# Agent attention with a routed expert layer: the planner that spreads side work beside the main tiles also counts GpSimd's instructions

## Chip, cores and metric

One core of a Trainium2 chip runs the whole program. The metric is device time in microseconds (us) of one execution, lower is better.

## What is computed

The reference first does attention through 49 agent vectors, then an expert layer on its output. Sizes: 4 batches of 10048 tokens, width 128; 4 groups of 4 experts, hidden width 1024.

```python
def _attn_ref(q, k, v, agents):
    a2k = sm(agents, k)              # softmax(scale * agents @ k^T), 49 x 10048
    agent_v = a2k @ v
    q2a = sm(q, agents)              # 10048 x 49
    return (q2a @ agent_v)
...
def _moe_ref(x, w_group, w_expert, w1, w2):
    g_logits = x @ w_group
    g_idx = np.argmax(g_logits, axis=1)
...
        e_logits = xg @ w_expert[g]
        e_idx = np.argmax(e_logits, axis=1)
...
            h = np.maximum(xg[mask_e] @ w1[g, e], 0.0)
            ye = h @ w2[g, e]
            combined = g_w[mask_g][mask_e] * e_w[mask_e]
            out[tok_idx] = combined[:, None] * ye
```

## The kernel before, in words

A batch has 79 blocks of 128 tokens. They are worked in **tiles** of 4 blocks (512 tokens), 20 to a batch, by `run`, which takes a tile through eight **units**. A unit is `first` (two matmuls into `ph`, a ScalarE relu into `hh`, and on VectorE the remainder `hl`, since every fp32 value is carried as two fp16 parts) and, eight units later (`LAG`), `second`, twelve matmuls into `po`. At a tile's end VectorE scales `po` into `oo`, and SyncE writes it out. A tile assumes one main expert for the whole batch; the tokens of other experts of the last batch are gathered and done at the end in 17 "taken" tiles (`er`, `ets`, indirect DMA on GpSimd's queue).

All other work is done by generators called **lanes**, which `run` advances between the units of the main tiles. TensorE's instructions from a lane keep the place in which they were written (`pe.pin`); the other engines' are ordered by the scheduler.

- Lane `f` finishes the queries of batch 0 (chunks of 8 blocks), lane `a` makes the agents of the next batch, lane `q` its queries and routing, lane `o` prepares the taken tiles.
- A key chunk in `a` and a query chunk in `q` and `f` begin with `split_load`: ScalarE writes `xh`, the fp16 part of 1024 columns, and GpSimd writes the remainder `xl` in pieces of 256 columns (four instructions a chunk). The scores' matmuls (`agh,xh`, `agl,xh`, `agh,xl`) then need both. There are two buffers each of `xh` and `xl`.
- Later steps of `q` make `rows` (ScalarE, with GpSimd's remainder), of `a` the values (`S`, `sh` and GpSimd's `sl`, VectorE's `vl`). Lane `q` ends with routing, which is VectorE's alone but for a few small matmuls: `oh`, `rm`, `rc`, then the count `cnt`, the main expert's number `mainid`, the loads `w1f` and `w2f`, `output_weight`, and `weights_of`, which fills `wbuf` for the next batch.

How far a lane is driven is decided by counted work. `Counted` wraps an engine and adds to `work[i]`, for each instruction, a fixed cost and a cost per element (nanoseconds, as written by the author). `advance` takes the dot product of what a step added with the weights `WA` and adds it to the lane's `done`; it goes on until `done` reaches the lane's total (`WORK`) times the elapsed part of its span (`SPAN_A`, `SPAN_Q`, `SPAN_F`, in batches: 0.3 is three tenths through batch 0's tiles). GpSimd is not wrapped before the change, so its instructions count nothing.

Of the kernel before, what the change touches and what calls it, by code (L numbers as in the profile page):

```python
# [79 lines left out]
SPAN_Q = {1: (0.53, 0.96), 2: (1.25, 1.78), 3: (2.1, 2.66)}  # L80
SPAN_O = (2.66, 2.92)
SPAN_F = (0.0, 0.52)
WA = (0.3, 1.0, 0.3)
WORK = {"a": 38e3, "q": 42e3, "o": 37.5e3, "f": 38e3}


def const_pack():
# [50 lines left out]

def build(ctx, tc, qT, kT, v, agT, wr, w1, w2, cpk, out):
    nc = tc.nc  # L140
    pool, sync = nc.gpsimd, nc.sync
    work = np.zeros(3)
    pe = Counted(nc.tensor, work, 0, 4.0, 0.42)
    vec = Counted(nc.vector, work, 1, 65.0, 1.04)
    act = Counted(nc.scalar, work, 2, 100.0, 0.83)

    const = ctx.enter_context(tc.tile_pool(name="const", bufs=1))
    stg = ctx.enter_context(tc.tile_pool(name="stg", bufs=4))
# [1060 lines left out]
    def advance(lane, part):  # L1209

        while lane["gen"] and lane["done"] < lane["total"] * part:
# [4 lines left out]
            if x == "end":  # L1216
                lane["gen"] = None
            lane["done"] += float(np.dot(work - w, WA))

    def lane(kind, b, gen, span):  # L1220
        lanes.append(dict(kind=kind, b=b, gen=gen, start=span[0], end=span[1], total=WORK[kind], done=0.0))

# [91 lines left out]
```

## Time and profile before

| | before |
|---|---|
| median of 3 runs (lowest to highest) | 976.26 us (974.47 to 979.38) |
| the profiled execution's own time | 972.96 us |
| its span, first to last instruction | 971.2 us |
| TensorE matmul / weight load, busy | 93% / 75% |
| VectorE, ScalarE, GpSimd, busy | 78%, 65%, 49% |
| mean granted TensorE clock | 0.983 of 2.4 GHz |

Busy shares are of the whole span. A matmul's shown duration includes its way through a pipeline, so TensorE can be shown busy while it starts fewer matmuls than it could; the counts beside the busy times tell that apart.

### The profile page before, as it was taken

What the parts mean: (1) busy time and instruction counts of PE and PEld (TensorE: products, weight loads), DVE (VectorE), ACT (ScalarE), POOL (GpSimd) and SP (SyncE); (2) the same over time, 40 slices, a digit from 0 to 9 for tenths busy, and PEclk for the clock granted to TensorE, in tenths of its full rate; (3) what the DMA queues carried; (4) which work ended last, traced back from release to release, by engine and by line L of the source; (5) the groups of instructions that cost most, each with busy time, mean ns of one, the idle gap of its engine ahead of it and who ended that gap; (6) DMA issues with size and microseconds to landing.
All of it is one profiled execution on the core that took longest, in us unless ns stands there. A gap on an engine that the chain in (4) does not pass through costs nothing.

```text
span 971.2 us, 31446 instructions
## 1 busy us (share of the span) xinstructions
PE 907.4 (93%) x13191; PEld 724.5 (75%) x13191; DVE 762.1 (78%) x1467; ACT 633.3 (65%) x1144; POOL 473.3 (49%) x776
## 2 busy tenths in 40 slices
PE   4979989899999999999889999999899999999996
PEld 3857767687877788887677878877777777777765
DVE  5589988977698987769989776699998766665653
ACT  5467677689757788885668678755455555555542
POOL 4243375388106428620552265300005578888886
PEclk9979989989999999999999999999999999999998
DMA  8863245352048535201883241014503643443311
GB/s 292 236 196 109 84 132 177 107 169 73 24 143 291 169 110 148 64 25 56 283 255 100 81 132 42 24 48 149 164 24 118 216 153 123 129 130 115 121 70 47
DMA packets 104423, 124.58 MB, mean 128 GB/s; under 512 B 6743, under 2 KB 88152, under 8 KB 101328
## 3 DMA queue, kind: packets, MB, share of 16 engines
q1 hardware_dynamic: 99920, 116.57, 38.1%
q0 software_dynamic: 4352, 5.91, 2.2%
q8 instruction: 105, 1.72, 0.7%
q14 instruction: 46, 0.38, 0.1%
HBM read 89.01 MB, written 33.75 MB: 126 GB/s over the span
## 4 chain that ended last, share of the span: by engine, by line
PE 37%; DVE 14%; POOL 4%; DMA 3%; issue 2%; ACT 1%; SPq 0%; POOLq 0%; DVEq 0%; ACTq 0%
PE po L131 19%; PE ph L131 13%; DVE hl L131 6%; PE at L131 6%; DMA xf<-kT 2%; POOL out L1128 1%; POOL er L1091 1%; DVE oo L131 1%; POOL gap L1107 1%; DMA er<-erow,gidx 1%; POOL xl L241 1%; DVE oh L131 1%; DMA wbuf<-wall 1%; DVE oa L131 0%; ACT hh L131 0%
## 5 line engine op out<-in xcount | busy, mean ns | idle before, releaser
L131 DVE SCALAR_TENSOR_TENSOR hl<-ph,hh 128x512 f16<-128x512 f32 (+1 forms) x656 | 435.7, 681 | 134.1 <-ACT hh L131 132.4
L131 PEld LDWEIGHTS <-hh 128*128 128x128 f16 x5200 | 425.3, 98 | 146.2 <-issue 3.3
L131 ACT ACTIVATE hh<-ph 128x512 f16<-128x512 f32 (+1 forms) x656 | 379.5, 594 | 188.2 <-PE ph L131 180.4
L131 PE MATMUL po<-wbuf,hh 128*128 128x128 f16 x4816 | 470.5, 220 | 0.0
L131 PE MATMUL po<-wbuf,hl 128*128 128x128 f16 x2408 | 435.7, 220 | 0.7 <-DVE hl L131 0.7
L131 PE MATMUL ph<-et,wbuf 98*128 98x512 f16 (+1 forms) x1040 | 306.1, 379 | 5.9 <-DVE hl L131 5.1
L241 POOL TENSOR_TENSOR xl<-xf,xh 128x256 f16<-128x256 f32 x292 | 195.6, 702 | 184.8 <-ACT xh L131 182.8
L131 PEld LDWEIGHTS <-hl 128*128 128x128 f16 x2600 | 254.1, 98 | 2.2 <-DVE hl L131 0.9
L1091 POOL DMA_INDIRECT er<-erow,gidx x68 | 69.7, 1025 | 124.5 <-DVE any L131 111.4
L131 PEld LDWEIGHTS <-wbuf 98*128 98x128 f16 x1216 | 94.0, 99 | 22.4 <-issue 12.9
L131 ACT ACTIVATE xh<-xf 128x1024 f16<-128x1024 f32 x80 | 83.2, 1045 | 30.5 <-PE at L131 18.2
L388 POOL TENSOR_TENSOR sl<-S,sh 128x147 f16<-128x147 f32 (+1 forms) x90 | 42.6, 500 | 94.5 <-ACT sh L131 88.4
L1128 POOL DMA_INDIRECT out<-oo,sidx x68 | 67.7, 996 | 23.8 <-DVE oo L131 12.6
L131 PE MATMUL at<-agh,xl 128*128 128x49 f16 x592 | 60.5, 188 | 11.0 <-POOL xl L241 10.1
L610 POOL TENSOR_TENSOR rows<-ef,rows 128x147 f16<-128x147 f32 (+2 forms) x117 | 46.6, 427 | 48.5 <-ACT rows L131 46.5
L131 PEld LDWEIGHTS <-xh 128*128 128x128 f16 x1264 | 60.7, 100 | 11.2 <-ACT xh L131 10.0
L131 PEld LDWEIGHTS <-xl 128*128 128x128 f16 x632 | 53.1, 99 | 16.3 <-POOL xl L241 15.3
L131 PE MATMUL at<-agh,xh 128*128 128x49 f16 x592 | 60.9, 188 | 1.9 <-ACT xh L131 1.7
L131 PE MATMUL at<-agl,xh 128*128 128x49 f16 x592 | 60.6, 188 | 0.0
L131 PE MATMUL ph<-ets,wbuf 98*128 98x512 f16 x176 | 53.1, 385 | 0.8 <-DMA wbuf<-wall 0.8
L1107 POOL MEMSET gap<- 128x320 f16 x136 | 52.4, 385 | 0.3
L131 DVE TENSOR_TENSOR oo<-po,cw 128x512 f32<-128x512 f32 x65 | 44.0, 676 | 5.0 <-PE po L131 5.0
(265 smaller groups left out, 1035.9 us busy)
## 6 DMA issues: line engine op xcount, KB each, us to landing
xf<-kT SPq DMA_DIRECT2D x36, 512.0 KB, 5.6
vf<-v SPq DMA_DIRECT2D x36, 512.0 KB, 5.1
xf<-qT SPq DMA_DIRECT2D x36, 512.0 KB, 4.0
out<-oo SPq DMA_DIRECT2D x62, 256.0 KB, 3.0
wbuf<-wall SPq DMA_DIRECT2D x11, 1024.0 KB, 5.0
wsg<-wall SPq DMA_DIRECT2D x6, 1024.0 KB, 6.8
erow<-rows SPq DMA_DIRECT2D x3, 1975.0 KB, 8.9
w1f<-w SPq DMA_DIRECT2D x7, 512.0 KB, 3.7
```

Of the source, the lines that this page charges most:

```text
L131: y = f(*a, **k)
L241: pool.tensor_sub(out=xl[:, y], in0=xf[:, y], in1=xh[:, y])
L388: pool.tensor_sub(out=sl[0:m, w], in0=x[:, j], in1=sh[0:m, w])
L610: (vec if early else pool).tensor_sub(out=rows[:, w, NA:2 * NA], in0=ef[:, y], in1=rows[:, w, 0:NA])
L1091: ins = pool.indirect_dma_start(out=er[:, q], out_offset=None, in_=erow[b][:, :], in_offset=bass.IndirectOffsetOnAxis(ap=place(b, j * w + ...
L1107: tc.keep_in_program_order(pool.memset(gap, 0.0))
L1128: ins = pool.indirect_dma_start(out=out, out_offset=bass.IndirectOffsetOnAxis(ap=place(x["b"], x["j"] * n + q)[1], axis=0), in_=o[:, q], i ...
```

## The change

GpSimd is wrapped by `Counted` as well (130 ns an instruction and 2.1 ns an element), with weight 0.5 in `WA`. A key chunk's `split_load` then counts for more than its scores, a step of pure VectorE routing for the same as before but against a larger total. The totals of `a`, `q` and `f` are raised; a count made while the program is built gives, as work actually done, 37.4e3 in `a` before and 56.6e3 after, 41.4e3 and 60.6e3 in `q`, 39.6e3 and 52.3e3 in `f`, so each total stands to the work done as it did. Lane `o` has no GpSimd work, and nothing moves in it or behind it. No instruction is added or removed; what moves is when each lane's steps are issued among the units.

```diff
-WA = (0.3, 1.0, 0.3)
-WORK = {"a": 38e3, "q": 42e3, "o": 37.5e3, "f": 38e3}
+WA = (0.3, 1.0, 0.3, 0.5)
+WORK = {"a": 57.4e3, "q": 61.5e3, "o": 37.5e3, "f": 50.2e3}
...
-    pool, sync = nc.gpsimd, nc.sync
-    work = np.zeros(3)
+    sync = nc.sync
+    work = np.zeros(4)
...
+    pool = Counted(nc.gpsimd, work, 3, 130.0, 2.1)
```

The first place is GpSimd (POOL) during batch 0, where lane `f` ends (`xl` and `rows` of query chunks) while lane `a` of batch 1 begins (`xl` of key chunks). Before, with the line of the instruction itself:

```order
L241 TENSOR_TENSOR xl<-xf,xh 128x256 x7
L241 TENSOR_TENSOR xl<-xf,xh 128x128
L241 TENSOR_TENSOR xl<-xf,xh 128x256 x4
L610 TENSOR_TENSOR rows<-ef,rows 128x3x49 x2
L610 TENSOR_TENSOR rows<-ef,rows 128x2x49
L241 TENSOR_TENSOR xl<-xf,xh 128x256 x20
L610 TENSOR_TENSOR rows<-ef,rows 128x3x49 x2
L610 TENSOR_TENSOR rows<-ef,rows 128x49
L241 TENSOR_TENSOR xl<-xf,xh 128x256 x7
```

After, the same place (all of GpSimd's counted instructions now carry the wrapper's line):

```order
L131 TENSOR_TENSOR xl<-xf,xh 128x256 x11
L131 TENSOR_TENSOR xl<-xf,xh 128x128
L131 TENSOR_TENSOR xl<-xf,xh 128x256 x4
L131 TENSOR_TENSOR rows<-ef,rows 128x3x49 x2
L131 TENSOR_TENSOR rows<-ef,rows 128x2x49
L131 TENSOR_TENSOR xl<-xf,xh 128x256 x12
L131 TENSOR_TENSOR rows<-ef,rows 128x3x49 x2
L131 TENSOR_TENSOR rows<-ef,rows 128x49
L131 TENSOR_TENSOR xl<-xf,xh 128x256 x11
```

Between the last two groups of `rows`, which belong to lane `f`, stood five key chunks (twenty pieces), and now three. On TensorE, the stretch from the first to the tenth group of batch 1's key scores held 16 units of main tiles, and holds 24.

The second place is VectorE (DVE) in the routing of batch 1, at the end of batch 0, from the count of tokens per expert (`cnt`) to the main expert's number (`mainid`). Before:

```order
L131 TENSOR_REDUCE cnt<-oh 128x16
L131 SCALAR_TENSOR_TENSOR hl<-ph,hh 128x512
L131 SCALAR_TENSOR_TENSOR code<-at,cp 128x16
L131 TENSOR_SCALAR zz<-lg 128x80
L131 TENSOR_REDUCE top<-code 128x1
L131 TENSOR_TENSOR rx<-lg,oh 128x1280
L131 SCALAR_TENSOR_TENSOR hl<-ph,hh 128x512 x3
```

After:

```order
L131 TENSOR_REDUCE cnt<-oh 128x16
L131 TENSOR_SCALAR zz<-lg 128x80
L131 TENSOR_TENSOR rx<-lg,oh 128x1280
L131 SCALAR_TENSOR_TENSOR hl<-ph,hh 128x512 x2
L131 SCALAR_TENSOR_TENSOR code<-at,cp 128x16
L131 RECIPROCAL zr<-zz 128x80
L131 TENSOR_REDUCE top<-code 128x1
```

Fewer `hl`, that is fewer units of main tiles, stand among the routing instructions. From the first routing row (`oh<-lg` over 80 columns) to the first `wbuf` remainder VectorE's order holds 25, 31 and 32 `hl` for batches 1, 2 and 3 before, and 17, 21 and 22 after; up to `cnt` alone 9, 9 and 9 before, 7, 9 and 8 after.

## Rows read from the trace of the kernel before

**Rows 1.** The page's head: span, then engines' busy time and share.

```profile
span 971.2 us, 31446 instructions
PE 907.4 (93%) x13191; PEld 724.5 (75%) x13191; DVE 762.1 (78%) x1467; ACT 633.3 (65%) x1144; POOL 473.3 (49%) x776
```

**Rows 2.** Busy time (and instructions) in stretches, granted clock, DMA.

```profile
core 0: us, PE busy (x) PEld busy (x) DVE busy (x) ACT busy (x) POOL busy (x), PEclk, DMA share, GB/s
120.00:160.00 40.00, 36.25 (x612) 28.72 (x609) 34.58 (x71) 30.37 (x55) 28.47 (x46) 0.91 0.52 152
...
440.00:475.00 35.00, 34.29 (x445) 26.41 (x443) 33.67 (x72) 20.86 (x37) 6.49 (x10) 1.00 0.48 147
...
632.00:735.00 103.00, 99.10 (x1255) 76.25 (x1253) 101.22 (x213) 51.44 (x90) 0.00 (x0) 1.00 0.29 93
...
780.00:870.00 90.00, 90.00 (x1152) 70.89 (x1151) 60.13 (x91) 51.49 (x88) 80.07 (x115) 1.00 0.42 139
```

**Rows 3.** PE and its weight loads (PEld), longest waits, 120 to 160 us.

```profile
PEld L131 <- POOL xl L241: 5.7, 14, 0.6
PE at L131 <- POOL xl L241: 3.6, 12, 0.5
```

**Rows 4.** The same view, 186 to 206 us.

```profile
PEld L131 <- POOL xl L241: 2.9, 4, 1.5
...
PEld L131 <- ACT xh L131: 0.8, 1, 0.8
```

**Rows 5.** Stretches of five us around both drops of the clock.

```profile
135.00:140.00 5.00, 3.54 (x62) 2.57 (x60) 4.93 (x14) 2.89 (x6) 3.39 (x6) 0.85 0.33 97
140.00:145.00 5.00, 4.41 (x39) 2.90 (x37) 4.04 (x7) 2.79 (x5) 4.60 (x8) 0.50 0.53 135
...
190.00:195.00 5.00, 2.06 (x26) 1.30 (x27) 4.51 (x10) 2.61 (x6) 4.70 (x7) 0.81 0.52 166
195.00:200.00 5.00, 5.00 (x54) 4.16 (x53) 4.30 (x9) 3.37 (x7) 4.50 (x9) 0.50 0.65 174
```

**Rows 6.** PEld's waits for GpSimd, 206 to 262 us.

```profile
PEld L131 <- POOL xl L241: 1.5, 4, 0.5
...
PEld L131 <- POOL rows L610: 1.0, 2, 0.8
```

**Rows 7.** The same view, 475 to 580 us.

```profile
PEld L131 <- POOL xl L241: 1.5, 4, 0.4
```

**Rows 8.** One chunk on GpSimd and on ScalarE, timelines of 119 to 150 us.

```profile
144.45 2.56 POOL L241 TENSOR_TENSOR xl<-xf,xh 128x256 f16<-128x256 f32 x4 [0.40 <-ACT xh L131]
...
143.33 1.05 ACT L131 ACTIVATE xh<-xf 128x1024 f16<-128x1024 f32 x1
```

**Rows 9.** GpSimd's `xl` alone in stretches: busy (count), clock, DMA.

```profile
186.00:206.00 20.00, 9.12 (x11) 0.83 0.43 124
206.00:262.00 56.00, 19.42 (x30) 1.00 0.28 83
300.00:345.00 45.00, 20.01 (x32) 1.00 0.69 225
```

**Rows 10.** VectorE's timeline in the routing of batch 1.

```profile
263.40 0.99 DVE L131 TENSOR_TENSOR oh<-lg 128x800 f16<-128x800 f32 x1 [0.35 <-ACT lg L131]
...
274.39 1.47 DVE L131 TENSOR_REDUCE cnt<-oh 128x16 f16<-128x1280 f16 x1
...
278.06 1.88 DVE L131 SCALAR_TENSOR_TENSOR hl<-ph,hh 128x512 f16<-128x512 f32 x3
279.86 0.23 DVE L131 TENSOR_SCALAR main<-code,top 128x16 f32<-128x16 f32 x1
...
297.70 0.68 DVE L131 TENSOR_TENSOR wbuf<-at,wbuf 128x512 f16<-128x512 f32 x1
```

**Rows 11.** All engines in that stretch, columns as in group 2.

```profile
263.40:297.70 34.30, 32.52 (x396) 24.66 (x394) 33.22 (x71) 20.57 (x35) 5.54 (x8) 1.00 0.42 125
```

**Rows 12.** PE's wait for `cnt`, 262 to 300 us.

```profile
PE at L131 <- DVE cnt L131: 1.1, 1, 1.1
```

## The prediction

> **What bounds the kernel now.** I read the busy shares first, then stretches, then what TensorE waited for, then the clock.
>
> The head of the page says that TensorE is the bound on the whole: 907.4 us of a 971.2 us span, with VectorE next at 762.1 and GpSimd far behind at 473.3 [rows 1]. An average like that hides stretches with other limits, so the stretches come next [rows 2]. The calm one is 780 to 870 us: 1152 matmuls in 90.0 us with VectorE only two thirds busy, so 0.078 us is the price of a mean main-tile matmul when nothing holds TensorE. A unit has 14 of them (two into `ph`, twelve into `po`), which makes 1.09 us a unit. Against that price the other stretches can be judged: 440 to 475 us has 445 matmuls, worth 34.8 us of its 35.0, and VectorE is busy for 33.67; 632 to 735 us has 1255, worth 98.0 of 103.0, with VectorE at 101.22. These two are the routing ends of batches 2 and 3 (the second with lane `o` behind it); the engines are level in the first, and VectorE sets the pace in the second.
>
> The stretch 120 to 160 us is another case: GpSimd is busy for 28.47 of 40 us and the clock stands at 0.91 [rows 2]. There TensorE's weight loads waited 5.7 us, in 14 waits, for GpSimd's `xl`, and its matmuls 3.6 us in 12 of the same waits [rows 3]. I count the weight loads' figure, since a matmul's shown end lies behind its real one. From 186 to 206 us, where lane `q` of batch 1 starts beside lane `a`, they waited 2.9 us for `xl` and 0.8 us for ScalarE's `xh` [rows 4]. Behind each of these waits the granted clock is at 1.2 GHz for a while. The means 0.85 and 0.50 in two stretches of 5 us stand for 1.5 + 5.0 = 6.5 us at half speed; 0.81 and 0.50 stand for 1.9 + 5.0 = 6.9 us [rows 5]. Just ahead of the first fall TensorE was shown busy for 3.54 of 5 us, ahead of the second for 2.06. Half of the time at the lower level is lost: 3.25 and 3.45 us. Later the same waits are smaller: 1.5 and 1.0 us between 206 and 262 [rows 6], 1.5 us between 475 and 580 [rows 7].
>
> **The change, part by part.** The number of instructions stays. What moves is the issue of lane steps: those with GpSimd work take more of the lane's span, those without take less.
>
> *Where two lanes draw on GpSimd.* A key chunk needs 1.05 us of ScalarE and then 2.56 us of GpSimd [rows 8]. From the first to the tenth group of batch 1's key scores, ten chunks cost GpSimd 25.6 us, and the end of lane `f` adds to that. TensorE's order held 16 units there, 16 x 1.09 = 17.4 us and the small scores matmuls beside; it now holds 24, which is 26.2 us. So GpSimd was the slower engine in that stretch, and TensorE is afterwards. The most that can be saved is 5.7 + 3.25 = 8.95 us. The first chunk still waits for its first piece, and lane `f`'s chunks still come in lumps; I take nine tenths, 8.1 us. The lower bound is nothing, if the lumps alone made the waits.
>
> At the start of lane `q` the most is 2.9 + 0.8 + 3.45 = 7.15 us. Here I take two thirds, 4.7 us: lane `a`'s value steps, which load VectorE, are also pushed together in that place, and VectorE was busy for 4.51 of 5 us just there [rows 5]. The lower bound is again nothing. In the later stretches the most is 1.5 + 1.0 + 1.5 = 4.0 us and I take 60%, 2.4 us, since only single waits stand there. Sum of the gains: 8.1 + 4.7 + 2.4 = 15.2 us taken, 20.1 at most.
>
> A point that speaks against this: one `xl` piece costs 20.01/32 = 0.625 us where keys run alone, 19.42/30 = 0.647 us between 206 and 262, but 9.12/11 = 0.83 us from 186 to 206 [rows 9], where value steps run beside. The Trainium skill has a rule for it (SBUF — State Buffer, section "SBUF: two separate sides"): GpSimd and a VectorE instruction with two SBUF inputs take the same pair of ports by turns, each for a whole instruction. By that rule, and by the row at 186 to 206, spreading lane `q` over lane `a`'s value steps would leave the second gain at nothing; by the row at 206 to 262 it costs almost nothing. I take the latter for most of lane `q`.
>
> *Where VectorE alone has the lane.* Routing counts as before, but against a total that is 46% larger, so it is driven through in fewer units. VectorE's part of a unit is one `hl`: three of them start within 279.86 - 278.06 = 1.80 us, 0.60 each [rows 10]. TensorE's part is 1.09. Each unit that leaves the routing stretch therefore takes 0.49 us more from TensorE's load there than from VectorE's. In batch 1 eight leave (25 to 17), in batches 2 and 3 ten each (31 to 21 and 32 to 22).
>
> Batch 1 first. In the 34.30 us from the first routing row to the first `wbuf` remainder, VectorE is busy for 33.22, and TensorE's 396 matmuls are worth 30.9 [rows 11]; VectorE leads by 2.3 us. After: 33.2 - 8 x 0.60 = 28.4 against 30.9 - 8 x 1.09 = 22.2, a lead of 6.2, so 3.9 us more. Batch 2 by the stretch of 440 to 475: 33.7 - 6.0 = 27.7 against 34.8 - 10.9 = 23.9, 3.8 us more where none was lost. Batch 3 by the stretch of 632 to 735: 101.2 - 6.0 = 95.2 against 98.0 - 10.9 = 87.1, a lead of 8.1 where it was 3.2, 4.9 us more. The top of this cost is 12.6 us. Its bottom is nothing: TensorE can run ahead of VectorE (`hl` is wanted eight units later, and there are six PSUM banks and ten buffers), and behind batches 1 and 2 come key chunks, with hardly any VectorE work, in which VectorE can catch up. What that lead can't cover is `cnt`: TensorE's one small matmul on it stands in program order and holds everything behind it, all later units. It waited 1.1 us [rows 12]; up to `cnt` VectorE's order has nearly as many `hl` as before while TensorE reaches it two to five units earlier. I take 2 us for each of batches 1 and 2 and, because lane `o` follows and leaves VectorE no room, the whole 4.9 for batch 3: 8.9 us.
>
> The loads of `w1f` and `w2f` are issued from `mainid`, which stays a fixed chain behind `cnt`; they land while the rest of routing covers them, and I cost that at nothing. That cover, `cnt` to the first `wbuf` remainder, is 23.3 us now [rows 10] and some 5 us less afterwards; were it gone, the first weight matmul would wait for the loads, a wait that takes the place of VectorE's and lies in the 3.9 us above.
>
> **Sum.** -15.2 + 8.9 = -6.3 us, on the profiled execution 973.0 to 966.7. The median of the runs shown lies 3.3 us above that execution, so I carry the difference over: 976.3 - 6.3 = 970.0 us.
>
> **The rivals.** A measurement of this kernel tells about 0.5%, here 4.9 us, from no change.
>
> 1. *The ends take back what the starts give: no change.* If the lead covers nothing, the ends cost 12.6 and the balance is -2.6, 973.7 us. If the starts keep half of their waits (7.6 gained), it is +1.3, 977.6. For it: VectorE at 97 to 98% in the routing of batches 1 and 3 [rows 2, 11]. Against it: TensorE lost nothing at batch 2's end with VectorE at 96%. The port rule of the section "SBUF: two separate sides" belongs here too; with the second gain at nothing the sum is -1.6, 974.7 us. Chance 0.32 together.
>
> 2. *Slower, by the clock at the routing ends.* The waits for `cnt` and `hl` come so close together that the granted clock falls there, as it did behind the `xl` waits, for about 6.7 us a time, 3.35 us lost. Three such falls cost 10 us, and where the waits are that close the lead has covered nothing: 976.3 - 15.2 + 12.6 + 10.0 = 983.7 us. It decides from the third fall on; with two the sum is +4.1. For it: both falls now came behind a row of short waits [rows 5]. Against it: at 632 to 735 us VectorE already sets the pace, and the clock stays at 1.00 [rows 2]. Chance 0.15. The Trainium skill (TensorE: Matmul & The Clock Gate, section "HAM oscillation — how this bites in real kernels") tells of a kernel whose clock drops at every wait for operands; by that, this rival would be the rule, and the trace agrees at two places out of the several where TensorE waits.
>
> 3. *The change does less than it says.* GpSimd's order comes from the scheduler, and two buffers of `xl` let it start a chunk early anyway; then starts and ends both move little and the time stays within 0.5%. It is part of rival 1's band; its chance is within the 0.32.
>
> My forecast, starts mostly cured and ends half covered, has 0.53.
>
> **How the numbers follow.** Faster by over 0.5% (under 971.4): the forecast, 0.53. Within 0.5%: 0.32. Slower: 0.15. The predicted time is 970. Its own range is 962 to 973. The whole range goes from 958 (18 of the 20.1 us gained, ends covered) to 983 (rival 2).
>
> **What would show it.** Right: TensorE's waits for `xl` between 120 and 206 us fall from 9.4 us (with `xh`) to about 2, the clock has no half-speed stretch there, and the ten key chunks of batch 1 are spread over about 35 us. In the routing of batch 1, first routing row to first `wbuf` remainder takes about 28 us instead of 34.3, and `cnt` is waited for by 2 to 4 us in each batch. From the taken tiles on (after about 760 us before) everything has the same length. Wrong: waits for `xl` that stay at several us, a clock at 1.2 GHz beside a routing end, or waits for VectorE (`cnt`, `hl`, `dw`) that sum to over 12 us more than now.

## The result: slower by 1.4%

| | before | after |
|---|---|---|
| median of 4 runs (lowest to highest) | 975.37 us (973.62 to 979.38) | 990.85 us (988.88 to 991.14) |
| span of the profiled execution | 971.2 us | 989.3 us |

The ratio of the two is 1.0136, with a 95% interval of 1.0103 to 1.0169. The forecast was 970 us with a range of 958 to 983, so the sign was wrong and the time lies outside the range. Seven runs on record, of the kernel before and of some told below, took 1170 to 4002 us and are left out of every ratio.

The head of the changed kernel's page (answers to [rows 1]) shows no engine with more work. VectorE and ScalarE do what they did; only the span is longer.

```profile
span 989.3 us, 31389 instructions
...
PE 914.3 (92%) x13191; PEld 728.3 (74%) x13191; DVE 757.7 (77%) x1467; ACT 632.9 (64%) x1144; POOL 475.8 (48%) x776
```

Stretches of the changed kernel, with the columns of [rows 2]. The first answers to 120 to 160 us there: more matmuls than the 612 of before, and the clock stays at its upper level. The rest is the start of lane `q` of batch 1, the answer to [rows 5].

```profile
120.00:160.00 40.00, 36.97 (x653) 30.25 (x652) 36.85 (x77) 30.32 (x56) 27.58 (x46) 1.00 0.51 151
...
190.00:195.00 5.00, 2.25 (x33) 1.53 (x31) 5.00 (x13) 2.59 (x6) 4.72 (x7) 0.98 0.57 174
195.00:200.00 5.00, 5.00 (x72) 4.14 (x71) 2.88 (x6) 2.52 (x4) 0.13 (x1) 0.68 0.96 291
200.00:205.00 5.00, 2.37 (x35) 1.90 (x33) 3.75 (x7) 3.44 (x7) 4.31 (x8) 1.00 0.77 205
205.00:210.00 5.00, 4.61 (x55) 3.87 (x55) 2.27 (x3) 3.34 (x6) 1.20 (x4) 0.66 0.29 97
...
215.00:220.00 5.00, 3.22 (x47) 2.31 (x45) 2.35 (x8) 3.22 (x7) 5.00 (x10) 0.87 0.24 43
220.00:225.00 5.00, 5.00 (x72) 4.40 (x71) 2.72 (x4) 4.07 (x7) 2.28 (x5) 0.79 0.53 172
```

Three times TensorE idles for 1.8 to 2.8 of 5 us, and each time the granted clock is at 1.2 GHz for a while behind it. By the clock column (what is missing to 1.00, times 5 us) the three cost 0.1 + 1.6, 1.7 and 0.65 + 1.05 us, together 5.1, where the one fall of before cost 3.45. What TensorE waited for there (186 to 232 us, waits with their times and the longest) had no row before the change:

```profile
PE at L131 <- POOL sl L131: 7.2, 3, 3.0
```

`sl` is GpSimd's remainder of lane `a`'s value step. GpSimd's timeline (start, duration) has four `xl` pieces of a query chunk ahead of it.

```profile
190.28 3.68 POOL L131 TENSOR_TENSOR xl<-xf,xh 128x256 f16<-128x256 f32 x4 [2.49 <-ACT xh L131]
193.92 1.21 POOL L131 TENSOR_TENSOR sl<-S,sh 128x147 f16<-128x147 f32 x3
```

ScalarE's `sh`, from which `sl` is made, started at 191.10 us by ScalarE's timeline and took half a microsecond:

```profile
191.10 0.52 ACT L131 ACTIVATE sh<-S 128x392 f16<-128x392 f32 x1
```

That order alone isn't new. Before the change the two stood in it as well, at nearly the same times:

```profile
190.59 3.67 POOL L241 TENSOR_TENSOR xl<-xf,xh 128x256 f16<-128x256 f32 x4 [0.30 <-ACT xh L131]
194.23 1.21 POOL L388 TENSOR_TENSOR sl<-S,sh 128x147 f16<-128x147 f32 x3
```

What is new is how soon TensorE wants it. By the two traces, the first piece of `sl` of the second to the seventh value chunk (eight blocks of lane `a`'s values) was done 3.9 to 11.5 us ahead of TensorE's first product with it; with the change it is done 0.05 to 0.6 us ahead, and nothing is left to cover a delay. Between two value chunks TensorE's order had 4 units of main tiles each time, and has mostly 3.

The other place is the ends. VectorE's timeline in the routing of batch 1, which answers to [rows 10]: from the first routing row to the first `wbuf` remainder it takes 302.30 - 276.72 = 25.6 us where it took 34.3.

```profile
276.72 0.99 DVE L131 TENSOR_TENSOR oh<-lg 128x800 f16<-128x800 f32 x1 [0.35 <-ACT lg L131]
...
286.51 1.48 DVE L131 TENSOR_REDUCE cnt<-oh 128x16 f16<-128x1280 f16 x1
...
302.30 0.68 DVE L131 TENSOR_TENSOR wbuf<-at,wbuf 128x512 f16<-128x512 f32 x1
```

And the stretches around the ends of the changed kernel: the last query steps ahead of batch 3's routing, that routing, and what follows it.

```profile
625.00:656.00 31.00, 31.00 (x513) 25.41 (x512) 20.40 (x33) 23.87 (x48) 9.46 (x20) 1.00 0.10 28
...
656.04:685.76 29.72, 28.68 (x346) 21.67 (x345) 28.52 (x65) 15.98 (x29) 0.00 (x0) 1.00 0.25 75
690.00:720.00 30.00, 23.43 (x251) 16.86 (x250) 27.63 (x61) 9.68 (x16) 0.00 (x0) 0.83 0.53 182
```

Read the third busy column: VectorE is busy for two thirds of the query steps (20.40 of 31.00) and for 96% of the routing. The change took units of main tiles from the second and gave them to the first. Behind the routing TensorE waits for two results of VectorE in lane `o` that place the taken tokens, `inc` and `dw`, and the clock stands at 0.83, which is 10.2 us at half speed, 5.1 us lost. The waits of 650 to 735 us:

```profile
PE at L131 <- DVE inc L131: 3.5, 1, 3.5
PE at L131 <- DVE dw L131: 3.1, 1, 3.1
PE at L131 <- DVE cnt L131: 1.0, 1, 1.0
```

Where the time went can be read from when TensorE had done equal work. I priced each matmul at the lower quartile of the distance to the next start, over the matmuls of its form in seven traces, summed in order of start, and compared the times at which two traces reach the same share of the whole. All columns but the first two are differences to the kernel before, in us. The columns e10 (the change with the ends kept), e17 (before with squeezed ends) and e14 (`q` alone with the ends kept) are experiments told below.

| share of work | before at | after | e10 | e17 | e14 |
|---|---|---|---|---|---|
| 0.100 | 115.4 | +0.9 | -0.4 | +1.1 | +1.5 |
| 0.150 | 171.4 | -6.2 | -7.5 | -0.2 | +1.3 |
| 0.175 | 200.6 | -5.0 | -6.3 | -0.1 | -2.2 |
| 0.200 | 224.6 | +2.7 | -1.8 | -1.9 | -2.1 |
| 0.250 | 272.4 | +2.1 | -0.2 | -4.5 | -2.7 |
| 0.325 | 341.8 | +2.9 | -0.9 | +4.5 | -2.5 |
| 0.400 | 409.7 | +7.5 | +4.0 | +5.0 | -3.4 |
| 0.450 | 454.0 | +7.2 | +4.8 | +4.6 | -2.5 |
| 0.500 | 503.7 | +10.0 | +0.6 | +14.1 | -1.9 |
| 0.700 | 685.7 | +9.2 | -0.5 | +12.6 | -3.2 |
| 0.725 | 710.7 | +17.8 | +2.5 | +19.4 | -0.3 |
| 1.000 | 962.1 | +18.1 | +1.3 | +17.6 | -2.0 |

Each column is one execution (the medians of the two kernels lie 15.5 us apart, these 18.1), and the part up to 115 us, which no edit touches but for the first lane `f` steps, differs by up to 2 us; smaller steps are not read. With the change, 7.1 us are gained on the key chunks by 171 us. 7.7 are lost between 201 and 225 (start of lane `q`), 4.6 between 342 and 410 (lane `a` and the start of lane `q` for batch 2), 2.5 from 410 to 504, across the end of batch 2, and 8.6 at the end of batch 3. From 711 us on the two kernels run alike.

### The profile page after: what moved, and what is told of

Read it like the earlier page. It is cut to its first block, busy times and chain, and to the rows that moved or that the text cites. A ratio compares the mean times of both kernels' runs of the same rounds, so it can differ in the third digit from the quotient of the medians.

```text
span 989.3 us, 31389 instructions
## 1 busy us (share of the span) xinstructions
PE 914.3 (92%) x13191; PEld 728.3 (74%) x13191; DVE 757.7 (77%) x1467; ACT 632.9 (64%) x1144; POOL 475.8 (48%) x776
## 4 chain that ended last, share of the span: by engine, by line
PE 34%; DVE 7%; POOL 4%; DMA 3%; issue 1%; ACT 1%; POOLq 0%; ACTq 0%; SPq 0%; DVEq 0%
PE po L131 18%; PE ph L131 12%; PE at L131 4%; DVE hl L131 2%; POOL er L131 2%; DMA er<-erow,gidx 1%; POOL gap L131 1%; POOL out L131 1%; DMA wbuf<-wall 1%; POOL xl L131 1%; DVE oo L131 0%; DVE oa L131 0%; DMA vf<-v 0%; DMA wall<-wsg 0%; DVE oh L131 0%
## 5 line engine op out<-in xcount | busy, mean ns | idle before, releaser
L131 ACT ACTIVATE xh<-xf 128x1024 f16<-128x1024 f32 (+1 forms) x80 | 83.1, 1045 | 36.3 <-PE at L131 22.9
L131 POOL TENSOR_TENSOR rows<-ef,rows 128x147 f16<-128x147 f32 (+2 forms) x117 | 49.7, 451 | 45.1 <-ACT rows L131 42.0
L131 PEld LDWEIGHTS <-xh 128*128 128x128 f16 x1264 | 59.3, 99 | 13.3 <-ACT xh L131 11.5
L131 PE MATMUL at<-agh,xl 128*128 128x49 f16 x592 | 58.4, 188 | 9.4 <-POOL xl L131 9.2
L131 PE MATMUL at<-agh,xh 128*128 128x49 f16 x592 | 58.8, 188 | 3.4 <-ACT xh L131 3.4
L131 PE MATMUL at<-agl,xh 128*128 128x49 f16 x592 | 58.5, 187 | 0.0
L131 DVE SCALAR_TENSOR_TENSOR vl<-vf,vh 128x1024 f16<-128x1024 f32 (+2 forms) x33 | 38.7, 1172 | 13.2 <-ACT vh L131 11.8
```

Source lines behind the costliest of these rows:

```text
L131: y = f(*a, **k)
```

## The experiments

**One lane at a time, and half the weight.** In three kernels GpSimd counts in one lane only; the others keep the old totals. The edit for lane `f` (for `a` and `q` the letter and the totals differ):

```diff
-WORK = {"a": 57.4e3, "q": 61.5e3, "o": 37.5e3, "f": 50.2e3}
+WORK = {"a": 38e3, "q": 42e3, "o": 37.5e3, "f": 50.2e3}
...
-            lane["done"] += float(np.dot(work - w, WA))
+            lane["done"] += float(np.dot((work - w)[:3], WA[:3])) + (WA[3] * float(work[3] - w[3]) if lane["kind"] in "f" else 0.0)
```

> GpSimd's instructions count in lane f alone (its total 50.2e3); lanes a and q are driven as before. Two theories of the 15.5 us that the whole change cost: ENDS, that lane q's routing, driven through fewer units, costs about 13 of them (VectorE, waits behind it, and the clock after them); VALUES, that lane a's value steps, driven through fewer units and with GpSimd's sl queued behind lane q's xl, cost about half of them and the rest is the ends. Both expect little of lane f: between -4 and +2 us against before, since f ends while lane a begins and its two last query chunks come a little later on GpSimd.

> GpSimd counts in lane a alone (total 57.4e3), lanes f and q as before. ENDS: routing is untouched, so -4 to +2 us. VALUES: TensorE waits for sl appear as in the whole change (8 us of them there, three falls of the clock between 190 and 230 us), and the time rises by 5 to 9 us.

> GpSimd counts in lane q alone (total 61.5e3), lanes f and a as before. ENDS: +11 to +16 us, with the waits for cnt, inc and dw and the falls of the clock at the end of batch 2's tiles as in the whole change. VALUES: +5 to +8 us, and hardly a wait for sl, since lane a's value steps keep their spacing.

The fourth halves the weight everywhere:

```diff
-WA = (0.3, 1.0, 0.3, 0.5)
-WORK = {"a": 57.4e3, "q": 61.5e3, "o": 37.5e3, "f": 50.2e3}
+WA = (0.3, 1.0, 0.3, 0.25)
+WORK = {"a": 47.7e3, "q": 51.75e3, "o": 37.5e3, "f": 44.1e3}
```

> GpSimd counts at weight 0.25 in all three lanes (totals 47.7e3, 51.75e3, 44.1e3, which stand to the work done as before). If the cost grows evenly with the weight, as both theories have it: +6 to +9 us. If half the weight already cures the waits for xl and the ends still fit under the tiles: -4 to +2 us.

Measured against the kernel before: `f` alone 1.0011 (0.9988 to 1.0033), `a` alone 1.0066 (1.0043 to 1.0089), `q` alone 1.0210 (1.0167 to 1.0253), half the weight 1.0010 (0.9990 to 1.0030). `a` alone came out as VALUES has it: routing stands where it stood before (`cnt` behind 131, 255 and 394 `hl`), and TensorE waits 4.7 us for `sl` from 186 to 232 us. So a part of the loss doesn't need squeezed ends. Half the weight puts `cnt` behind 136, 262 and 402 `hl`, about two thirds of the way to the 139, 267 and 406 of the change, and brings no change of the time: the loss doesn't grow evenly with the weight. Lane `q` alone costs more than the whole change, and more than either theory had, so the parts don't add up: they meet. With `q` alone TensorE's longest account is `xl`, 17.2 us in 45 waits against 10.1 in 28 before:

```profile
PE at L131 <- POOL xl L131: 17.2, 45, 1.4
```

The added ones come behind the routing: 3.7 us from 285 to 345 us and 6.2 from 485 to 530, where the kernel before has none and 1.1. SyncE's queue in that kernel shows the key loads of the next batch (`xf<-kT`) right behind `w1f`, whose issue needs `mainid` (before the change they stand behind it too, but start at 283.65 us):

```profile
286.98 0.37 SPq L838 DMA_DIRECT2D w1f<-w  x1
287.55 0.40 SPq L839 DMA_DIRECT2D w2f<-w  x1
288.06 0.52 SPq L922 DMA_DIRECT2D out<-oo  x1
288.68 6.44 SPq L223 DMA_DIRECT2D xf<-kT  x4
```

**Is it the queue?** Three kernels issue the next batch's first three key loads ahead of the routing: the changed one, the one with `q` alone, and the kernel before as a control.

```diff
+        for ci in range(3 if b < LB else 0):
+            yield from load_only("k", b + 1, ci)
         yield from routing(b, 0, NTP)
         yield from main_of(b, NTP)
```

> The whole change, and in lane q, ahead of the routing of batches 1 and 2, the first three key chunks of the next batch are loaded (the loads xf<-kT, which otherwise stand on SyncE's queue behind w1f, whose issue waits for mainid). QUEUE, the theory now: at the end of a batch the routing's later mainid holds SyncE's queue, so the next keys come late, TensorE waits for xh and xl and the clock falls: of the 15.5 us some 6 to 9 come back, that is +6 to +10 us against before. VECTORE, the rival: the ends are long because VectorE's routing has fewer units beside it; the loads change nothing, +14 to +17 us.

> GpSimd counted in lane q alone, with the same three early key loads. QUEUE: the greater part of the 20 us comes back, +4 to +10 us against before, with no long wait for xh and few for xl at 295 to 345 and 485 to 530 us and no fall of the clock there. VECTORE: +18 to +21 us.

> The kernel before with the same early key loads, as a control. QUEUE: its keys come in time already, -3 to +1 us. VECTORE: 0.

Measured: 1.0137 (1.0097 to 1.0177) for the changed kernel, 1.0081 (1.0055 to 1.0107) for `q` alone, 0.9991 (0.9975 to 1.0006) for the kernel before. With `q` alone the late loads were 1.3 of the 2.1%. In the whole change they are nothing that can be measured in time, and the queue falls as the cause of its loss. By equal work the early loads do move something there: from 454 to 504 us the trace gains 1.9 us where the changed kernel's loses 2.8, but from 272 to 300 us it loses 4.0 instead of 0.4, where TensorE now waits 1.9 us for `w1f`.

**`sl` on another engine.** GpSimd's `sl` goes to VectorE, counted as before so that the lanes are driven alike.

```diff
-                pool.tensor_sub(out=sl[0:m, w], in0=x[:, j], in1=sh[0:m, w])
+                work[3] += 130.0 + 2.1 * NA * (j.stop - j.start)
+                nc.vector.tensor_sub(out=sl[0:m, w], in0=x[:, j], in1=sh[0:m, w])
```

> The whole change, with the value steps' sl on VectorE, in the same pieces and counted as before, so that the lanes are driven alike and only the engine differs. SL-QUEUE: TensorE waits 8.5 us for sl because GpSimd has a whole query chunk of xl before it, and three falls of the clock follow: these go, 6 to 10 us come back, less up to 3 us for 20 us more work on VectorE, so +7 to +11 us against before. SPACING, the rival: the value steps stand too close for any engine; the waits move from sl to VectorE and the time stays at +14 to +18 us.

Two runs are too few for a ratio. They took 1022.0 and 1023.6 us where the kernel before beside them had a median of 1007.9, 14 and 16 us more, which is what SPACING expected. By equal work its trace loses 5.1 us from 201 to 225 us, where the changed kernel's lost 7.7; from 171 us on, so that the first of the three waits lies within, it is 1.9 against 8.9. TensorE then waits for VectorE's `sl` instead (2.8 us in 5 waits from 186 to 232 us, 5.0 in 6 in all). But what is gained there isn't kept: at 640 us this kernel is 9.1 us behind the kernel before, the changed one 9.2. So GpSimd's order is part of the loss at that place, and curing that place doesn't shorten the whole.

**The ends kept.** The part of lane `q` from routing on is counted 1.86 times and the total raised to match. Routing then has the same share of the lane as before the change, and `cnt` stands behind as many `hl` in VectorE's order as before. The second kernel does so for batch 3 alone.

```diff
+        if b in (1, 2, 3):
+            FACTOR["q", b] = 1.8556
         yield from routing(b, 0, NTP)
...
-            lane["done"] += float(np.dot(work - w, WA))
+            lane["done"] += float(np.dot(work - w, WA)) * FACTOR.get((lane["kind"], lane["b"]), 1.0)
...
-        lanes.append(dict(kind=kind, b=b, gen=gen, start=span[0], end=span[1], total=WORK[kind], done=0.0))
+        lanes.append(dict(kind=kind, b=b, gen=gen, start=span[0], end=span[1], total=WORK[kind] + (16.4e3 if kind == "q" and b in (1, 2, 3) else 0.0), done=0.0))
```

> The changed kernel with routing, output weights and weights of lane q counted 1.86 times (total raised to match), so that cnt stands behind as many units as before the change (131, 255, 394 in VectorE's order). Theory 'ends': the 10 us and more that the change loses from the routing of batch 1 on come from routing spread over fewer units; most of it returns, ratio to the kernel before 1.001 to 1.006, waits for inc and dw at 1 us or less, no half-speed stretch at 490 and at 700 to 715. Rival 'starts': the waits for sl and the three clock falls of batch 0 carry the loss; then 1.010 to 1.014, with the sl waits still near 8 us.

> The same for batch 3 alone. Theory 'ends': the part of the loss that lies behind the routing of batch 3 (marks moved by 7 us from the third routing's key scores to the last weights) returns, 5 to 7 us, ratio 1.006 to 1.009, and the half-speed stretches at 700 to 715 go. Rival 'starts': 1.012 to 1.015, unchanged.

Measured: 0.9990 (0.9971 to 1.0010) with all ends kept, 1.0064 (1.0042 to 1.0086) with the last one. The whole loss is gone, a little more than expected, and about half of it with batch 3's end alone. In the first kernel the waits of 640 to 735 us no longer have `inc` or `cnt`, and in the stretch of the routing, 40 us again, TensorE is shown busy throughout:

```profile
PE at L131 <- DVE dw L131: 2.5, 1, 2.5
```

```profile
635.00:675.00 40.00, 40.00 (x490) 30.56 (x488) 39.32 (x88) 22.72 (x40) 0.00 (x0) 1.00 0.25 81
...
695.00:700.00 5.00, 4.35 (x11) 1.84 (x12) 4.69 (x13) 2.96 (x5) 0.00 (x0) 0.55 1.07 335
700.00:705.00 5.00, 5.00 (x50) 3.35 (x49) 4.68 (x10) 2.88 (x5) 0.00 (x0) 0.77 0.44 136
```

Two details of the expectation missed: `dw` is waited for by 2.5 us, as before the change, not 1; and a half-speed stretch is still there, 4.5 + 2.3 = 6.8 us. It goes with the +3.0 that the e10 column has between 686 and 711 us (the e14 column has +2.9).

**More room for lane `a`.** The value steps get their old distance by a longer span, without and with the ends kept.

```diff
-SPAN_A = {1: (0.3, 0.7), 2: (0.95, 1.42), 3: (1.72, 2.15)}
+SPAN_A = {1: (0.27, 0.74), 2: (0.95, 1.51), 3: (1.72, 2.15)}
```

> The changed kernel with lane a's spans made longer (0.27 to 0.74 for batch 1, 0.95 to 1.51 for batch 2), so that the value steps stand about as far apart as before the change and the key chunks keep their spread. Theory: the sl waits come from value steps that stand too close; they fall from 8.5 us to under 3, the clock does not fall at 190 to 225 us, and 4 to 8 us return, ratio 1.006 to 1.010. Rival: the sl waits come from lane q's four xl pieces ahead of them in GpSimd's order, wherever the value steps stand; waits and time as with the change, 1.012 to 1.016.

> Both edits together. If the theories of the two hold and add up: 0.992 to 0.998, below the kernel before, since the key chunks' gain stays and neither the value steps nor the ends pay for it. If the spreading itself gains nothing: 1.000 to 1.004. If neither edit reaches the loss: above 1.010.

Measured: 1.0100 (1.0074 to 1.0127) and 0.9985 (0.9964 to 1.0005). In the first of the two TensorE's wait for `sl` between 186 and 232 us falls from 7.2 to 0.7 us (GpSimd's `rows` comes up instead, 2.7), and by equal work the stretch from 201 to 225 us costs 3.8 us instead of 7.7. The clock still falls there (0.66 from 190 to 195 us, 0.79 from 205 to 210), which the expectation had ruled out. So the distance of the value steps is part of that loss. With the ends kept the sum stays at no change, so the two gains don't add up.

**Are squeezed ends enough?** This is the kernel before, with GpSimd counted nowhere. The edit is that of the ends, with 0.5389 for 1.8556 and -8.8e3 for 16.4e3, so that `cnt` stands exactly where the change puts it in VectorE's order (139, 267 and 406 `hl` ahead of it). Beside it run three that keep the ends: with GpSimd counted in `q` alone, in `f` and `q`, and in all lanes with lane `a` ending at 0.74 and 1.51 but starting at 0.3.

> The kernel before, GpSimd counted nowhere, with the routing part of lane q counted 0.54 times (total lowered to match), so that cnt stands where the change puts it (139, 267, 406 in VectorE's order). Theory 'ends': squeezing the routing alone brings the loss, 1.008 to 1.022, with half-speed stretches behind the routing of batches 2 and 3 and waits for cnt, inc and dw. Rival: the loss needs GpSimd counted; 0.998 to 1.004.

> GpSimd counted in lane q alone, with q's routing part counted 1.86 times so that cnt stands behind as many units as before the change (131, 255, 394). The run with q alone lost 2.1%. Theory 'ends': that loss is the routing driven through in fewer units and the loads behind it; with the ends as before, what stays is the smoother start of q (4 to 6 us gained in batch 1's q, by the times at which TensorE had done equal work): ratio 0.992 to 0.999. Rival: counting GpSimd in q costs by itself, through query chunks that stand farther apart; 1.010 to 1.020.

> The same with GpSimd counted in f too, not in a. Theory: like the run before it, 0.991 to 0.999, since f alone gave no change (1.001); if f's wider chunks run into lane a's keys, 1.000 to 1.006.

> The whole change with the ends kept and lane a ending later (0.74 and 1.51) but starting where it did. Theory: the 7 to 8 us gained on the key chunks of batch 1 stay, and the value steps give back less of it than in the run with the ends alone (0.999): 0.990 to 0.998. Rival: what the key chunks gain is given back within the lane wherever it ends: 0.997 to 1.003.

Measured: the squeezed kernel 1.0175 (1.0143 to 1.0206); `q` alone with the ends kept 0.9954 (0.9934 to 0.9975); with `f` 0.9977 (0.9955 to 1.0000); all lanes with the longer `a` 1.0037 (1.0016 to 1.0058), above both its expectations. Squeezing the routing brings a loss of this size by itself. At the end of batch 3 it looks the same: the waits (640 to 735 us) and the clock behind them are much like those of the change:

```profile
PE at L131 <- DVE inc L131: 3.2, 1, 3.2
PE at L131 <- DVE dw L131: 1.6, 1, 1.6
PE at L131 <- DVE cnt L131: 1.2, 1, 1.2
```

```profile
702.00:707.00 5.00, 4.48 (x26) 2.81 (x26) 4.46 (x17) 1.79 (x3) 0.00 (x0) 0.50 0.17 52
707.00:722.00 15.00, 13.42 (x149) 10.04 (x147) 14.30 (x35) 5.39 (x9) 0.00 (x0) 0.84 0.61 192
```

At the ends of batches 1 and 2 it is another. By equal work the squeezed kernel loses 9.0 us (272 to 342) and 9.5 (454 to 504) there, the changed one 0.8 and 2.8. Its waits for `xl` are those of `q` alone, 17.2 us in 45:

```profile
PE at L131 <- POOL xl L241: 17.1, 45, 1.4
```

In both kernels lane `a` isn't spread, and its key chunks meet loads that stand behind `w1f` (from 289.60 us on here); in the changed kernel these loads come later still, from 295.48 us on, but its key chunks are spread. That the loads make the 9.0 and 9.5 wasn't tried in this kernel.

And the one edit of routing turns `q` alone from the worst kernel (1.021) into the best (0.995), faster than both kernels of the study. Its page's head:

```profile
span 970.3 us, 31438 instructions
...
PE 907.0 (93%) x13191; PEld 724.0 (75%) x13191; DVE 760.5 (78%) x1467; ACT 633.5 (65%) x1144; POOL 475.4 (49%) x776
```

**More of it?** From that best kernel, routing counted 2.4 times in place of 1.86, and, in a second kernel that keeps the 1.86, lane `a` ending later (0.74 and 1.51).

```diff
-            FACTOR["q", b] = 1.8556
+            FACTOR["q", b] = 2.4
...
-total=WORK[kind] + (16.4e3 if
+total=WORK[kind] + (26.8e3 if
```

> The best kernel so far (GpSimd counted in q alone, ends kept, ratio 0.995) with the routing part counted 2.4 times in place of 1.86: cnt stands 4 to 6 units earlier than before the change (127, 249, 389), so routing is spread over more units than ever. Theory 'VectorE is the bound at the ends': more room there is worth something again, 0.990 to 0.996. Rival: before the change TensorE lost hardly anything at the ends, so there is nothing left to win, and the query steps, which come closer, lose some of q's start: 0.996 to 1.003.

> The same kernel with lane a, which doesn't count GpSimd, ending at 0.74 and 1.51 in place of 0.70 and 1.42, so that key chunks and value steps both stand a tenth to a fifth farther apart. If lane a's closeness costs time by itself: 0.988 to 0.994. If what its steps gain is given back behind them, as with the whole change: 0.995 to 1.003.

Measured: 0.9954 (0.9935 to 0.9973) and 0.9969 (0.9953 to 0.9986). The first lies within what its theory expected, but the kernel it starts from had 0.9954 too, so more room for the routing changes nothing; more room for lane `a` is worth nothing either. So the price of the ends is one-sided: far fewer units than before cost time, and more than before bring nothing back.

## Why the prediction was wrong, step by step

*The key chunks.* Under "Where two lanes draw on GpSimd", the first term was 8.1 us; 7.1 were gained by 171 us. Between 120 and 165 us TensorE's matmuls waited 2.6 us for `xl`, its weight loads 3.4, where [rows 3] have 3.6 and 5.7, and the clock has no fall there. The mechanism was right.

*The start of lane `q`: the step that failed first.* The prediction took 4.7 us there and said: "The lower bound is again nothing." The bound was wrong. 7.7 us were lost, some 12 us from the forecast. The step named the reason (value steps pushed together just there) and priced it only as a smaller gain, on VectorE. What showed up was a chain through GpSimd, `S`, `sh`, `sl` and the products, with `xl` ahead of `sl` and no distance left to cover it. `q` alone, with lane `a` as before, does gain there: by equal work 3.7 us from 115 to 201 us in the e14 column, and nothing lost behind it. From 201 to 225 us more distance for the value steps halves the loss, and `sl` on VectorE takes a third of it. With a fixed span, what key chunks gain value steps pay.

*"In the later stretches".* 2.4 us were to be gained; from 342 to 410 us 4.6 were lost, where batch 2's lane `a` meets lane `q`. The e10 column loses 4.9 there too, so it isn't the ends, and the column in which lane `a` doesn't count GpSimd (e14) loses nothing. This points at lane `a`'s steps. That it is the chain through `sl` again isn't shown: TensorE's waits there are spread over `xl` (1.5 us), `mx` (1.1) and `at` (1.0), with 0.4 for `sl` (345 to 417 us).

*"Where VectorE alone has the lane".* The sum was 2 + 2 + 4.9 = 8.9 us, and the changed kernel's trace shows at these places 0.2 (225 to 342 us), 2.5 and 8.6, together 11.3. The direction was right. Routing took 25.6 us where 28 was forecast, and the `cnt` waits were 1.0 to 1.3 us each where 2 to 4 were. What was mis-sized is batch 3: the lead was priced, 4.9, and the clock left out. The waits for `inc` and `dw`, 6.6 us against the 2.5 for `dw` before, and 5.1 us lost at half speed, come to 9.2 and are about the 8.6. "I take 2 us for each" leaned on VectorE catching up in the key chunks behind. The kernel with the squeezed ends shows that this cover isn't sure: where key chunks aren't spread it loses 9.0 and 9.5 us at the ends of batches 1 and 2, and 6.8 at batch 3's.

*The loads of `w1f` and `w2f`, "I cost that at nothing".* TensorE waited 1.0 us for `w1f` in batch 1. That SyncE's queue holds the next batch's key loads behind them was left out. With `q` alone that is worth 1.3%; in the whole change, nothing measurable.

*Rival 2* had the sign, at a chance of 0.15, with three falls of the clock behind routing waits. Its place was half right: three falls stand at the start of `q`, behind GpSimd's `sl`, one at the end of batch 2 (0.82 from 490 to 495 us) and two at the end of batch 3. The Trainium skill (TensorE: Matmul & The Clock Gate, section "HAM oscillation — how this bites in real kernels") tells of a kernel whose clock drops at every wait for operands. The trace agrees at those places, but behind the `cnt` waits of batches 1 and 3 (1.3 and 1.0 us) the clock doesn't fall. *Rival 1* took back too little, since it let the start of `q` come out at nothing at worst. The rule on shared ports, weighed there, is not decided: an `xl` piece cost 8.56/10 = 0.86 us from 186 to 206 us against 0.83 before, too little to make the loss there.

*The sum.* Three gains of 15.2 us in all were forecast; by 410 us the change had lost 6.6 (from +0.9 to +7.5). The ends were put at 8.9 and came to some 11. So by place most of the miss is at the starts. By experiment it isn't so plain: giving the routing its old share back takes the whole loss away (0.9990), although 4.5 and 4.9 us are still lost from 201 to 225 and from 342 to 410 us, because that kernel gains 3.4 us from 410 to 504, where the changed one loses 2.5. What a place loses is not what its cure gives back.

What is settled: the whole change's loss needs the squeezed routing (1.0136, and 0.9990 with its old share), and batch 3's end is about half of that. Squeezed routing is enough for a loss of this size, through partly other waits. It isn't the only thing that costs: `a` alone loses 0.7% with the routing untouched. What is open: why keeping the ends also takes 3.2 us off the loss at the start of lane `q` (7.7 to 4.5). Query chunks stand closer there again, as before the change; that this is the reason was argued, not tried. Nor was the half-speed time at batch 3's end tried apart from the waits.

## What to carry to other kernels

A planner that spreads work by cost shares out a fixed span, so counting one more engine takes units from every step that doesn't use it. Before adding an engine's cost, ask which engine sets the pace in the steps that will shrink: GpSimd was at 49% on the whole, and the units went from steps with VectorE at 96% to steps with it at 66%. Bound each moved step on both sides, too: the neighbour that is pushed together can lose more than the spread one gains.

## What the runs showed that was not expected

In the runs with the early loads and with `sl` on VectorE the kernel before beside them had a median of 1007.9 us, against 975 to 979 beside all others. It isn't the chip alone: the chip of the same number had 977.6 us some 26 minutes later. The difference lies in the taken tiles: there the changed kernel with early loads starts 835 matmuls in 80 us at a granted clock of 1.00, where the changed kernel itself, in its own runs, started 1025, and the profile shows nothing that TensorE waits for. In the kernel before with early loads, from 760 us on:

```profile
PE po L131 <- issue: 18.3, 58, 1.1
```

The cause is open. Each ratio above is to the kernel before as it ran beside that kernel.
